# A planned two-layer transformer kernel: five groups of loads get other gates or places, and the order of work is planned anew with another price list

## The chip, the core and the metric

The kernel runs on one core of a Trainium2 chip. The core has a matrix engine (PE, with its weight loads shown apart as PEld), a vector engine (DVE), an activation engine (ACT), a general engine (POOL) and a queue engine (SP) that here issues every DMA. The metric is the device time of one execution in microseconds (us), the median of several.

## What is computed

Two sweeps of the same two layers over a sequence of 2048 tokens of width 576, all in bfloat16 at the edges:

```python
x = A_x                                              # 1 x 2048 x 576
for _ in range(2):
    y = layernorm(x)
    q, k, v = split(y @ wqkv)                        # 32 heads of 18
    p = softmax(where(0 <= i - j < 256, q k^T * 18**-0.5, -1e9))
    x = x + (p @ v) @ wo                             # sliding-block attention
    h = gelu_tanh(layernorm(x) @ w1 + b1)            # 576 -> 4608
    x = x + h @ w2 + b2                              # 4608 -> 576
```

## The kernel before

**Chunks and stages.** The 2048 tokens are cut in chunks of four tiles of 128 tokens; two sweeps give eight chunks, numbered k = 0 to 7. A chunk passes through: the first layernorm and a transpose of its tiles (`ln1_in`, `ln1`, written to `xnTa`), the q, k and v products (`qkv`), attention in eight groups of heads (`E0` for the first chunk, `E` for the others, cut in parts ea, eb and ec), the output product with the second layernorm and its transpose (`tail`, written to `xnTm`), and the MLP in three thirds of its 4608 hidden columns: `G_part` (first product and gelu: ga, gb, gc) and `mm2` (second product: ma, mb, mc). The MLP of chunk k-1 is woven with the attention of chunk k. A third of `w2` stays in `w2_sb` in two halves of 864 KB; `w1` goes through three slots, one slice of six column blocks each, of one load of 768 KB and two of 48 KB.

**The planner.** No order is written out by hand. Every instruction is added to a `Plan` as a task with its engine, the names it reads and writes, a cost, a latency (`lat`), for a DMA also a transfer time (`move`) and a number of descriptors (`desc`), and a priority. `Plan.schedule` then simulates the engines and at each step takes the task that can start first; among those of one starting time, the one of lowest priority number. A table `PL.nudge` adds a number to the priority of each stage by its name ("ga0" for the first third of chunk 0's MLP, "ga0+" for the weight loads that the stage issues, and so on). The order that comes out is the order of each engine's queue in the program; the engines then run it with semaphores, each strictly in its order. So the planned costs set the order, and never the time on the chip.

**DMAs and gates.** All DMAs are issued by SP, in the planned order. A load whose `reads` names something waits until that is written: this is a *gate*, though the load does not use the data. `dma_start_transpose` is a DMA that transposes a tile on its way: normalized tiles to `xnTa` and `xnTm`, and q and k tiles to `qT` and `kT`. Only chunk 0's normalized tiles and k tiles are transposed on PE (L738, L874). An SP instruction that waits holds all DMAs behind it.

**The start (the ramp).** SP loads token tiles 0 and 1, the q weights, tiles 2 and 3, the k weights, the v weights, then tiles 4 to 7. A DVE chain of fixed order (`PL.chain = "dv"`, L1149 to L1157) does the statistics of tile 0, half of tile 1's, the normalization of tile 0, the rest of tile 1's statistics, those of tile 2, then the normalization of tile 1, and so on. Then come `qkv` of chunk 0, its attention, and the first layernorm of chunk 1. PE fills planned gaps of over 0.4 us with products of zeros (`keep_warm`, L683).

**Names that the change touches.** The biases: `b1in` (a 36 x 128 view in `hT`) is loaded, transposed on PE (L1172) and copied to `b1col` (L1174); `b2bc` is loaded to all partitions. Both loads have the gate "k3", the fourth k tile of chunk 0. Gelu (L1086) reads `b1col`; POOL adds `b2bc` to `x_res` (L1092). Names used as gates: `k<i>` a transposed k tile, `v0h0` half of a v tile, `xa<i>` tile i of `xnTa`, `xm0_<i>` tile i of `xnTm` for an even chunk, `aq<g>` the attention output of head group g (L973), which is written once in each chunk. In the last chunk the third of `w2` that is used last goes to the place of `wqkv` (`w2x`).

Of the kernel before, what the change touches and what calls it, by code (L numbers as in the profile page):

```python
# [9 lines left out]
P = 128  # L10
# [176 lines left out]
class Plan:  # L187
# [75 lines left out]
    def schedule(self):  # L263
# [55 lines left out]
        served = {}  # L319
        n = len(self.tasks)  # L320
        while len(order) < n:
# [43 lines left out]
            if t.dma is not None:  # L365
# [15 lines left out]
                done = at + t.move  # L381
                for o in served:
                    if o != t.eng and served[o] > at:
                        both = min(t.move, served[o] - at)
                        served[o] += both
                        done += both
                served[t.eng] = done
                q.append((done - t.move, done, t.desc))
# [42 lines left out]
SWITCH = 0.095  # L431
TURN_FROM = 40.0
# [4 lines left out]
def build_kernel(nc, A_x, A_wqkv, A_wo, B_x, B_w1, B_b1, B_w2, B_b2, out):  # L437
# [42 lines left out]
    PL.nudge = {"": -230.72, "b": 275.87, "ea0.0": 68.12, "ea0.2": -36.73, "ea0.p0": 25.27, "ea0.p1": 8.39, "ea0.p2": 19.16,  # L480
# [168 lines left out]

    xin_load(0, 1)  # L650
    xin_load(1, 1)
    w_load(0)
    xin_load(2, 2)
    w_load(1)
    w_load(2)
# [660 lines left out]
```

## Time and profile before

| | |
|---|---|
| Median of 3 runs | 864.4 us (862.9 to 865.43) |
| The profiled execution's own time | 864.13 us |
| Its span, first to last instruction | 862.3 us |
| Granted PE clock, mean over the span | 0.998 |
| ACT busy | 593.2 us (69%) |
| DVE busy | 392.0 us (45%) |
| POOL busy | 377.9 us (44%) |
| DMA | 119.77 MB, 139 GB/s on average |

The profile is of one execution. Busy time is the time in which an engine has an instruction running; "PEclk" is the share of full clock that PE was granted. A timeline row gives the start, the duration, the engine, the line of the program, the operation with the tiles it writes and reads, and how many instructions were merged; in brackets stands the idle time before it and what ended it. Rows of stretches give the length, the busy time of each engine with its number of instructions, the granted clock, the share of the DMA engines and GB/s. In the chain of waits, each row says who waited, for whom, the total, the number of times and the longest.

### The profile page before, as it was taken

To read this page: it belongs to the slowest core of one execution; us is meant where nothing else is said; L and a number is where in the kernel's file an instruction comes from. 1 tells how busy PE (TensorE), PEld (TensorE's weight loads), DVE (VectorE), ACT (ScalarE), POOL (GpSimd) and SP (SyncE) were. 2 spreads that over 40 slices of the span, in tenths; PEclk is the share of its full clock that TensorE was granted. 3 is DMA by queue.
4 is the path that set the end of the run, shared out by engine and by line. 5 is a ranking of instruction groups with operands and counts; after the bars stand their busy time and mean duration, and the time that the engine had idled before them with its cause. 6 is when DMAs were issued, how large, how long until landed. Compare 5 with 4: busy or idle time off the path is not lost.

```text
span 862.3 us, 26990 instructions
## 1 busy us (share of the span) xinstructions
PE 848.7 (98%) x11578; PEld 520.5 (60%) x11578; DVE 392.0 (45%) x934; ACT 593.2 (69%) x741; POOL 377.9 (44%) x560
## 2 busy tenths in 40 slices
PE   8899999999999999999999999999999999999998
PEld 6556556656556565565655655656556656656656
DVE  7689424655228542384424832655224434243012
ACT  4796788768667588573875876737787589771730
POOL 4687544465135653264421863425454276222100
PEclk9999999999999999999999999999999999999999
DMA  7887435351583615957359443673536953355320
GB/s 192 197 193 142 124 125 148 109 163 44 166 181 107 163 43 166 204 93 169 90 151 218 92 139 125 116 177 98 173 112 119 289 155 105 126 166 146 120 83 28
DMA packets 181862, 119.77 MB, mean 139 GB/s; under 512 B 107440, under 2 KB 181744, under 8 KB 181744
## 3 DMA queue, kind: packets, MB, share of 16 engines
q1 hardware_dynamic: 181744, 118.05, 53.7%
q8 instruction: 91, 1.49, 0.7%
q14 instruction: 27, 0.22, 0.1%
HBM read 90.10 MB, written 2.36 MB: 107 GB/s over the span
## 4 chain that ended last, share of the span: by engine, by line
PE 87%; DMA 4%; DVE 4%; ACT 2%; issue 2%; SPq 1%; POOL 1%; POOLq 0%; DVEq 0%; ACTq 0%
PE ps L1076 31%; PE ps L781 27%; PE ps L784 9%; PE ps L840 8%; PE ps L909 6%; PE ps L956 4%; ACT pT L918 2%; DMA xnTm<-xn 2%; PE ps L800 1%; DMA xnTa<-xn 1%; DVE x_res L1019 1%; DVE xn L721 1%; DVE st_all L696 1%; SPq L633 1%; DMA wqkv<-in_A_wqkv_dram 1%
## 5 line engine op out<-in xcount | busy, mean ns | idle before, releaser
L939 POOL TENSOR_SCALAR_AFFINE_SELECT pT<-pT 128x512 bf16<-128x512 bf16 (+1 forms) x368 | 282.8, 789 | 250.1 <-ACT pT L918 244.9
L918 ACT ACTIVATE pT<-ps 128x1024 bf16<-128x1024 f32 (+1 forms) x384 | 345.1, 974 | 58.0 <-PE ps L909 57.6
L1076 PE MATMUL ps<-xnTm,w_sb 64*128 64x512 bf16 x2592 | 290.5, 376 | 0.9 <-DVE x_res L1019 0.3
L1086 ACT ACTIVATE hT<-ps,b1col 128x512 bf16<-128x512 f32 x276 | 167.4, 687 | 173.9 <-PE ps L1076 173.4
L1076 PEld LDWEIGHTS ps<-xnTm,w_sb 64*128 64x128 bf16 x2592 | 128.8, 94 | 142.5 <-issue 6.4
L781 PE MATMUL ps<-w_sb,hT 128*128 128x288 bf16 x1506 | 201.1, 287 | 0.0
L1019 DVE TENSOR_TENSOR x_res<-ps,x_res 128x288 f32<-128x288 f32 x224 | 100.0, 450 | 188.2 <-PE ps L781 162.1
L781 PEld LDWEIGHTS ps<-w_sb,hT 128*128 128x128 bf16 x1506 | 139.9, 98 | 51.5 <-issue 15.6
L840 PE MATMUL ps<-wqkv,xnTa 64*128 64x288 bf16 x1296 | 91.7, 283 | 1.6 <-DVE x_res L1019 1.1
L967 DVE STREAM_TRANSPOSE oq<-ps 128x512 f32<-128x512 f32 x64 | 45.8, 716 | 98.9 <-PE ps L956 98.0
L784 PE MATMUL ps<-w_sb,hT 128*32 128x288 bf16 x2424 | 83.7, 287 | 0.1
L861 DVE CAST qn<-ps 128x288 bf16<-128x288 f32 x120 | 49.0, 450 | 76.4 <-PE ps L840 68.8
L840 PEld LDWEIGHTS ps<-wqkv,xnTa 64*128 64x128 bf16 x1296 | 61.3, 94 | 31.4 <-issue 2.7
L784 PEld LDWEIGHTS ps<-w_sb,hT 128*32 128x32 bf16 x2424 | 62.2, 97 | 13.6 <-issue 4.2
L909 PE MATMUL ps<-qT,kT 32*128 32x384 bf16 (+2 forms) x1216 | 64.1, 276 | 2.8 <-ACT pT L918 2.3
L696 DVE BATCH_NORM_STATS2 st_all<-x_res 128x6 f32<-128x288 f32 (+1 forms) x128 | 53.4, 442 | 6.7 <-DMA x_res<-in_A_x_dram 5.8
L709 POOL TENSOR_SCALAR vtmp<-mv_all 128x1 f32<-128x1 f32 (+1 forms) x43 | 8.8, 204 | 107.7 <-DVE mv_all L700 105.3
L848 DVE CAST vA<-ps 128x288 bf16<-128x288 f32 x64 | 26.5, 450 | 63.2 <-PE ps L840 59.5
L1092 POOL TENSOR_TENSOR x_res<-x_res,b2bc 128x576 f32<-128x576 f32 x32 | 40.2, 1275 | 32.8 <-ACT hT L1086 32.8
L956 PE MATMUL ps<-pT,vA 128*20 128x384 bf16 (+2 forms) x1408 | 50.5, 276 | 0.2 <-DVE qn L861 0.2
L909 PEld LDWEIGHTS ps<-qT,kT 32*128 32x128 bf16 x1216 | 19.4, 92 | 42.8 <-issue 26.3
L781 PE MATMUL ps<-wo_sb,attT 128*128 128x288 bf16 x320 | 42.1, 287 | 0.3 <-DVE qn L861 0.3
(56 smaller groups left out, 465.1 us busy)
## 6 DMA issues: line engine op xcount, KB each, us to landing
w_sb<-in_B_w_dram SPq DMA_DIRECT2D x46, 864.0 KB, 6.0
w_sb<-in_B_w_dram SPq DMA_DIRECT2D x48, 768.0 KB, 4.7
w_sb<-in_B_w_dram SPq DMA_DIRECT2D x96, 48.0 KB, 4.4
wqkv<-in_A_wqkv_dram SPq DMA_DIRECT2D x3, 576.0 KB, 5.6
x_res<-in_A_x_dram SPq DMA_DIRECT2D x3, 576.0 KB, 5.7
wqkv<-in_B_w_dram SPq DMA_DIRECT2D x2, 864.0 KB, 6.3
out_dram<-x_res SPq DMA_DIRECT2D x12, 144.0 KB, 2.0
wo_sb<-in_A_wo_dram SPq DMA_DIRECT2D x4, 144.0 KB, 2.6
```

The source lines that it names most:

```text
L696: add("dve", lambda e, i=i, s=s: e.bn_stats(st_all[:, t, i, :], s[:, t, i * HB:(i + 1) * HB]), reads=res, writes=[f"st{t}_{i}"], cost=0.37 ...
L781: return e.matmul(bank(b)[:, 0:HB], lhs, rhs, start=start, stop=stop, skip_group_check=True)
L784: ins = e.matmul(bank(b)[32 * j:32 * j + 32, 0:HB], lhs[:, 32 * j:32 * j + 32], rhs, start=start, stop=stop, tile_position=(0, 32 * j), sk ...
L840: ins = e.matmul(bank(bs[o])[:, 0:HB], xnTa[r:r + 64, c, i * 128:(i + 1) * 128], wqkv[r:r + 64, c, col:col + HB], start=(c == 4), stop=(ph ...
L861: add("dve", lambda e, b=bs[o], dst=dst: e.tensor_copy(dst, heads_of(bank(b))), reads=[bs[o]], writes=[f"qn{sl}h{o}"], cost=0.375, lat=0.1 ...
L909: ins = e.matmul(two(bs[j // 2])[:, j % 2, col:col + nq * 128], k_of(T0 + so)[0][32 * j:32 * j + 32, g, :], qs[32 * j:32 * j + 32, g, qo * ...
L918: add("act", lambda e, h2=h2: e.activation(pT[:, sl, 2 * h2:2 * h2 + 2, lo:hi], two(bs[h2])[:, :, lo:hi], ACT.Exp, scale=SCALE), reads=[bs ...
L939: add("pool", lambda e, ap=ap, pat=pat, sgn=sgn, kind=kind: e.affine_select(ap, ap, pattern=pat, compare_op=(ALU.is_ge if kind == "d" else ...
L956: ins = e.matmul(bank(bo)[32 * j:32 * j + VW, qo * 128:(qo + nq) * 128], vA[:, (T0 + so) % VS, 8 * j + g, :], pT[:, sl, j, col:col + nq * ...
L1019: add("dve", lambda e: e.tensor_tensor(x_res[:, t, sl], bank(b)[:, 0:HB], x_old[:, t, sl], ALU.add), reads=[b] + ([f"xin{t}"] if first els ...
L1076: ins = e.matmul(bank(bks[i])[:, 0:n], w1_sb[r:r + 64, sls[i], col:col + 128], xnTm[r:r + 64, k % 2, c, 0:n], start=(c == 4), stop=(ph == ...
L1086: add("act", lambda e, ff=ff, hd=hd, bk=bk: e.activation(hd[:, 0:n], bank(bk)[:, 0:n], ACT.Gelu_apprx_tanh, bias=b1col[:, ff:ff + 1]), rea ...
```

## The change

It removes no arithmetic and adds none. It has six parts.

1. The three loads of the k weights go ahead of the load of token tiles 2 and 3.
2. The loads of both biases are moved from behind chunk 0's `qkv` (gate "k3") to a function `biases()` that is called after chunk 0's attention has been added (gate "aq1"); the PE transpose of b1 also waits for "aq7".
3. The second `w1` slice gets the gate of tiles 2 and 3 of `xnTa` in place of "v0h0", the third is moved to the MLP of chunk 0 with the gate of all four tiles of `xnTm` in place of "aq2".
4. The two halves of the first `w2` third get that same gate in place of "aq5" and "aq7".
5. The last `w2` third, in the place of `wqkv`, gets the gates "aq2" and "aq5" (of the last chunk).
6. The planner's price list: transposing DMAs get a longer latency and a shorter transfer, `w2` loads a shorter transfer, and a plain DMA of 500 descriptors or more that follows a transposing one while the queue is still busy is charged 0.8 more. With that the table of nudges is another; some of its entries (those of ea2, ea7, ga1 and ga6, for example) are those of before.

```diff
+                mv = t.move + (TURN_DMA if t.desc >= 500 and t.dma != "t" and turned.get(t.eng) and served.get(t.eng, 0.0) >= at else 0.0)
+                turned[t.eng] = t.dma == "t"
-                done = at + t.move
+                done = at + mv
...
+TURN_DMA = 0.8
...
-    PL.nudge = {"": -230.72, "b": 275.87, "ea0.0": 68.12, "ea0.2": -36.73, "ea0.p0": 25.27, "ea0.p1": 8.39, "ea0.p2": 19.16,
+    PL.nudge = {"": -92.05, "b": -19.76, "ea0.0": 28.56, "ea0.1": -4.45, "ea0.2": 114.56, "ea0.p0": -14.45, "ea0.p2": 33.51,
...
     w_load(0)
+    w_load(1)
     xin_load(2, 2)
-    w_load(1)
     w_load(2)
...
-            reads=rd, writes=[...], dma="t", ring=8, cost=1.3, lat=0.7, move=1.0, desc=640, prio=prio)
+            reads=rd, writes=[...], dma="t", ring=8, cost=1.3, lat=0.95, move=0.75, desc=640, prio=prio)
...
-                cls="w2", ring=NFH // WB, cost=0.55, lat=2.0, move=0.5 * WB,
+                cls="w2", ring=NFH // WB, cost=0.55, lat=2.0, move=0.4 * WB,
...
-                    reads=[f"qn{sl}h0", f"qn{sl}h1"], writes=[dn], dma="t", ring=8, cost=1.3, lat=1.1, move=1.3, desc=1024, prio=prio)
+                    reads=[f"qn{sl}h0", f"qn{sl}h1"], writes=[dn], dma="t", ring=8, cost=1.3, lat=1.4, move=1.0, desc=1024, prio=prio)
...
-    PL.stage = "b"
-    bb = Bank(FILL)
-    dma("sp", b1in, ..., reads=["k3"], writes=["b1i"], cls="b", ring=2, cost=0.5, prio=-1)
-    dma("sp", b2bc[:, :], ..., reads=["k3"], writes=["b2"], cls="b", ring=2, cost=0.5, prio=-1)
-    add("pe", lambda e: e.transpose(...), reads=["b1i", "ident"], writes=[bb], cost=0.1, lat=0.22, prio=5, alloc=[bb])
-    add("dve", lambda e: e.tensor_copy(b1col[:, :], ...), reads=[bb], writes=["b1"], cost=0.1, lat=0.14, prio=5)
...
+    def biases():
+        PL.stage = "b"
+        bb = Bank(FILL)
+        dma("sp", b1in, ..., reads=["aq1"], writes=["b1i"], cls="b", ring=2, cost=0.5, prio=-1)
+        dma("sp", b2bc[:, :], ..., reads=["aq1"], writes=["b2"], cls="b", ring=2, cost=0.5, prio=-1)
+        add("pe", lambda e: e.transpose(...), reads=["b1i", "ident", "aq7"], writes=[bb], cost=0.1, lat=0.22, prio=5, alloc=[bb])
+        add("dve", lambda e: e.tensor_copy(b1col[:, :], ...), reads=[bb], writes=["b1"], cost=0.1, lat=0.14, prio=5)
...
             PL.stage = f"ga{k - 1}"
+            if k == 1:
+                w1_load(-1, [f"xm0_{i}" for i in range(4)])
             G_part(k - 1, 0, b + 0.6)
         if k == 1:
-            w2_load(0, 1, ("aq5", "aq7"))
+            w2_load(0, 1, [[f"xm0_{i}" for i in range(4)]] * 2)
...
             if k == 0:
-                w1_load(-1, ["v0h0"])
-                w1_load(-1, ["aq2"])
+                w1_load(-1, ["xa2", "xa3"])
+                biases()
...
-            w2_load(2, b + 3, k=k - 1)
+            w2_load(2, b + 3, ("aq2", "aq5") if k == NK else None, k=k - 1)
```

More of the change, by code (lines that the diff above doesn't have):

```diff
@@ L319, in schedule @@
         served = {}
+        turned = {}
         n = len(self.tasks)
@@ L380, in schedule @@
                 at = max(served.get(t.eng, 0.0), st + t.cost + min(t.lat, 2.0))
-                done = at + t.move
+                mv = t.move + (TURN_DMA if t.desc >= 500 and t.dma != "t" and turned.get(t.eng) and served.get(t.eng, 0.0) >= at else 0.0)
+                turned[t.eng] = t.dma == "t"
+                done = at + mv
                 for o in served:
                     if o != t.eng and served[o] > at:
-                        both = min(t.move, served[o] - at)
+                        both = min(mv, served[o] - at)
                         served[o] += both
@@ L387, in schedule @@
                 served[t.eng] = done
-                q.append((done - t.move, done, t.desc))
+                q.append((done - mv, done, t.desc))
                 done += max(0.0, t.lat - 2.0)
@@ L744, in ln_norm_T @@
         add("sp", lambda e: e.dma_start_transpose(dst[:, :, i * 128:(i + 1) * 128], xn[:, sl, :]),
-            reads=rd, writes=[f"{dname}{i}"] + (["kx0", "kx1"] if dname == "xm1_" else []), dma="t", ring=8, cost=1.3, lat=0.7, move=1.0, desc=640, prio=prio)
+            reads=rd, writes=[f"{dname}{i}"] + (["kx0", "kx1"] if dname == "xm1_" else []), dma="t", ring=8, cost=1.3, lat=0.95, move=0.75, desc=640, prio=prio)
     w1n = [0]
@@ L774, in w2_load @@
             dma("sp", wt[:, WB * b:WB * b + WB, :], B_w2[f0 * P:(f0 + WB) * P, :].rearrange("(w p) d -> p w d", p=P),
-                reads=[gate[b]] if gate else [], writes=[f"{wn}{b}"] + ([f"w{w}{x}{h}" for w in "qkv" for x in "BC" for h in range(2)] + [f"w{w}A" for w in "qkv"] if wn == "w2x" else []), cls="w2", ring=NFH // WB, cost=0.55, lat=2.0, move=0.5 * WB,
+                reads=([gate[b]] if isinstance(gate[b], str) else gate[b]) if gate else [], writes=[f"{wn}{b}"] + ([f"w{w}{x}{h}" for w in "qkv" for x in "BC" for h in range(2)] + [f"w{w}A" for w in "qkv"] if wn == "w2x" else []), cls="w2", ring=NFH // WB, cost=0.55, lat=2.0, move=0.4 * WB,
                 desc=128 * WB, prio=prio)
@@ L1165, in build_kernel @@
     PL.part = ""
-    PL.stage = "b"
-    bb = Bank(FILL)
-    dma("sp", b1in, bass.AP(tensor=B_b1.tensor, offset=B_b1.offset, ap=[[P, NF], [1, P]]), reads=["k3"], writes=["b1i"], cls="b", ring=2,
-        cost=0.5, prio=-1)
-    dma("sp", b2bc[:, :], bass.AP(tensor=B_b2.tensor, offset=B_b2.offset, ap=[[0, P], [1, D]]), reads=["k3"], writes=["b2"], cls="b", ring=2,
-        cost=0.5, prio=-1)
-    add("pe", lambda e: e.transpose(bank(bb).bitcast(BF16)[:, 0:NF], b1in, ident[0:NF, 0:NF]), reads=["b1i", "ident"], writes=[bb],
-        cost=0.1, lat=0.22, prio=5, alloc=[bb])
-    add("dve", lambda e: e.tensor_copy(b1col[:, :], bank(bb).bitcast(BF16)[:, 0:NF]), reads=[bb], writes=["b1"], cost=0.1, lat=0.14, prio=5)
     PL.stage = ""
@@ L1197, in wo_load @@
             dma("sp", wo_sb[32 * j:32 * j + 16, 4, :], A_wo[r + 128:r + 144, :], reads=["aq0"], writes=[f"woB{j}"], cls="wo", cost=0.6)
+    def biases():
+        PL.stage = "b"
+        bb = Bank(FILL)
+        dma("sp", b1in, bass.AP(tensor=B_b1.tensor, offset=B_b1.offset, ap=[[P, NF], [1, P]]), reads=["aq1"], writes=["b1i"], cls="b", ring=2,
+            cost=0.5, prio=-1)
+        dma("sp", b2bc[:, :], bass.AP(tensor=B_b2.tensor, offset=B_b2.offset, ap=[[0, P], [1, D]]), reads=["aq1"], writes=["b2"], cls="b", ring=2,
+            cost=0.5, prio=-1)
+        add("pe", lambda e: e.transpose(bank(bb).bitcast(BF16)[:, 0:NF], b1in, ident[0:NF, 0:NF]), reads=["b1i", "ident", "aq7"], writes=[bb],
+            cost=0.1, lat=0.22, prio=5, alloc=[bb])
+        add("dve", lambda e: e.tensor_copy(b1col[:, :], bank(bb).bitcast(BF16)[:, 0:NF]), reads=[bb], writes=["b1"], cost=0.1, lat=0.14, prio=5)
     later = [k for k in range(2, NK) if CH[k][0] == 0]
```

140 rows, old and new, of the table add are left out of this document.

## Prediction

> **What bounds the kernel now.** I read the page's busy times first, then the busy time by stretches, the waits, and the timelines of PE, SP and ACT where PE idles.
>
> ```profile
> span 862.3 us, 26990 instructions
> ...
> PE 848.7 (98%) x11578; PEld 520.5 (60%) x11578; DVE 392.0 (45%) x934; ACT 593.2 (69%) x741; POOL 377.9 (44%) x560
> ```
>
> PE is the bound: 862.3 - 848.7 = 13.6 us without a matmul. By the stretches PE lacks 3.1 us in 0 to 20, 3.0 in 20 to 40, 1.2 in 40 to 60, 1.3 in 60 to 120 and, added up from the 20 us rows, 2.0 in all of 140 to 800. The last product ends at 859.4, so 2.9 us are the output's way out. A change of order can win little after 140 us; the ramp is where it is.
>
> ```profile
> 29.46 0.35 PE L909 MATMUL ps<-qT,kT 32*128 32x256 bf16 x8 [0.38 <-DVE mv_all L700]
> 30.72 0.34 PE L909 MATMUL ps<-qT,kT 32*128 32x384 bf16 x4 [0.91 <-ACT pT L918]
> 32.48 2.59 PE L784 MATMUL ps<-wqkv,xnTa 128*32 128x288 bf16 x40 [1.42 <-DMA xnTa<-xn]
> 34.86 0.77 PE L956 MATMUL ps<-pT,vA 128*20 128x384 bf16 x16
> 35.55 0.34 PE L909 MATMUL ps<-qT,kT 32*128 32x256 bf16 x8
> ```
>
> PE stands 1.42 us for a tile of chunk 1 that a transposing DMA brings; the scores of chunk 0 (35.55) stand in its queue behind that product. The clock falls meanwhile:
>
> ```profile
> 31.00:31.50 0.50, 0.06 (x4) 0.00 (x0) 0.48 (x2) 0.50 (x2) 0.07 (x1) 1.00 0.08 9
> 31.50:32.00 0.50, 0.00 (x0) 0.00 (x0) 0.00 (x0) 0.50 (x2) 0.50 (x1) 0.65 1.03 326
> 32.00:32.50 0.50, 0.02 (x4) 0.02 (x6) 0.00 (x0) 0.50 (x2) 0.50 (x1) 0.50 1.05 292
> ...
> 34.50:35.00 0.50, 0.50 (x16) 0.34 (x12) 0.00 (x0) 0.00 (x0) 0.50 (x2) 0.50 0.52 165
> 35.00:35.50 0.50, 0.50 (x20) 0.21 (x11) 0.37 (x1) 0.00 (x0) 0.10 (x1) 0.94 0.00 0
> ```
>
> The column before the last two is the granted clock: 0.50 from about 31.65 to 35.05. ACT pays:
>
> ```profile
> 29.85 2.92 ACT L918 ACTIVATE pT<-ps 128x768 bf16<-128x768 f32 x4 [0.56 <-PE ps L909]
> 35.95 23.16 ACT L918 ACTIVATE pT<-ps 128x768 bf16<-128x768 f32 x32 [3.18 <-PE ps L909]
> ```
>
> From 35.95 to 64.05 ACT idles 0.18 us: chunk 0's attention is bound by its exponentials. So the 3.18 us of ACT idle are on the path, not only PE's 1.42. SP shows why the tile was late:
>
> ```profile
> 21.66 0.60 SPq L633 DMA_DIRECT2D hT<-in_B_b_dram  x1
> 22.36 1.24 SPq L880 DMA_TRANSPOSE qT<-qn  x1
> 23.70 2.02 SPq L744 DMA_TRANSPOSE xnTa<-xn  x1
> 25.77 0.58 SPq L633 DMA_DIRECT2D b2bc<-in_B_b_dram  x1
> 26.45 2.52 SPq L744 DMA_TRANSPOSE xnTa<-xn  x2
> 29.02 0.57 SPq L633 DMA_DIRECT2D w_sb<-in_B_w_dram  x1
> 29.64 2.29 SPq L744 DMA_TRANSPOSE xnTa<-xn  x1
> ```
>
> The four tiles were normalized by 20.5 (DVE's and POOL's timelines), but stand behind w1's first slice, tiles 8 to 11, both biases and, the last one, w1's second slice. The chain of work that ended last takes the one issued at 27.70, which landed 4.74 us later.
>
> **The sum, part by part.**
>
> *Biases (part 2) and w1's second slice (part 3): -2.5.* The bias issues ahead of that tile cost 0.60 and 0.58 with gaps of 0.10 each: 1.38 us that SP gives back, and 153 KB less ahead of it. The 1.42 us wait all but goes. With it goes the slow clock: 40 products in 2.59 against 2 x 0.80 for 20 of the same kind at 38.69 and 41.44, so 0.99, and 0.11 on the P.V product (0.77 against 0.66). 1.4 + 1.1 = 2.5, of ACT's 3.18. Bounds: 0 if another DMA comes late in its place; -4.0 if the 0.38 + 0.91 + 0.20 us beside it go too (2.91 + 1.10). I take 2.5, since those are waits for ACT, which is busy then. What the biases now cost: two issues of 1.2 us after 41.8 (group 1's output), one PE transpose of 0.19 and a copy of 0.18 after 66.3; gelu first reads b1 at 90.31, POOL b2 at 91.14. Over 20 us of cover; without it, 0.2 plus the wait. w1's second slice, behind the tiles, is first used some 4 us into the MLP at 87: covered. SP is also rid of 1.77 us (w1's third slice, 49.13) and 0.97 (w2, 57.79 and 66.69) there.
>
> *k weights ahead of tiles 2 and 3 (part 1): +0.3.* 648 KB (0.66 MB) at the 329 to 334 GB/s of 4 to 8 us make 2.0: the tiles land near 10.0 where DVE now has them at 7.96; the k weights land 288 KB, 0.9 us, before 10.16. DVE's fixed chain puts tile 1's normalization (8.93) behind tile 2's statistics, so it slips 2 us, and q of tile 1 with it. Tile 2, which the first scores need, is normalized at 10.43 but transposed on PE only at 12.74, behind a product that waited for the k weights: 1.5 us of slack. q of tile 2 is copied out at 16.39, behind statistics of tiles 4 to 7 whose landing (13.28) doesn't move. Bounds: -0.9 (k weights earlier, all of it on the path) to +2.0; most of the slip is absorbed, so +0.3.
>
> *w1's third slice and w2's first third behind xnTm (parts 3, 4): 0.* At 86.7 SP now issues tiles 12 to 15 (576 KB, landed after 4.3 us, at 91.0). Behind them now come 864 + 1728 = 2592 KB, 2.65 MB. At 366 GB/s (row 96 to 98) they land at 98.3, at 272 (100 to 102) at 100.8. w2's first half is needed at 99.82, after 11.83 us of first products that start from the same tiles, the second some 0.8 later. It just fits, and both ends move with the tiles. Bounds 0 and +7.5, the first rival.
>
> *The last w2 third (part 5): 0.* Its loads go out at 671.94 and 679.25 and are used after 835; PE has no idle time in 660 to 700, so nothing is won.
>
> *The order found anew (part 6): -1.1.* In the ramp ACT also waits 0.67 and 0.56 for scores (27.79, 29.85); longer transposes in the plan make it put such products later: half of 1.23, -0.6. After 140 a quarter of the 2.0 idle, -0.5 (the largest is 1.07 before 389.47, for a tile of xnTm). What a new order does to PE's turns between kinds of product is not to be read; one turn costs 0.1: 20 products take 2.56 and 192 take 23.64 in the chain, so 2.56 - 20 x 0.123. Twenty turns more or fewer, of the chain's 756 pieces, bound it at +2.0 and -2.0; I take none.
>
> Sum: 864.13 - 2.5 + 0.3 - 1.1 = 860.8, against its own span 859.0 and 1.8 around it; the median of the runs lies 0.27 above the profiled one, which I leave. About 0.3% (2.6 us: 861.8 to 867.0) is what a measurement here tells from no change.
>
> **The rivals.**
>
> *Late MLP weights (slower).* Everything gathered behind xnTm meets the transposes of chunk 1's q and k. Such stretches ran at 147 (84 to 88) and 196 GB/s (96 to 100). At their mean, 172, the 2.65 MB take 15.4 us and land at 106.4: 5.8 us behind the need, and the clock's fall costs half of 3.4: 860.8 + 7.5 = 868.3. It decides below 2.65 MB / (100.6 - 91.0) = 276 GB/s. For it: no spare landing place; against: 366 and 358 GB/s (116 to 120) in weight loads alone, and 92 to 96 nearly free of DMA.
>
> *The gain is lost at the start.* Tiles 2 and 3 come 2.0 later and the first scores with them: 860.8 + 1.7 = 862.5, no change by the bound. For it DVE's fixed chain; against it the 1.5 us of slack.
>
> *The clock falls all the same.* PE is thinly used from 29.0 on, before the wait: 1.5 of the 3.4 us up to 31.65. If the wait goes and the fall stays, 1.1 is not won: 861.9. [...]
>
> *All small waits go too.* -4.0, +0.3, all of 1.23 and 0.8 of 2.0 idle: 858.4.
>
> *The new order turns more often.* 40 turns: 864.8. Nothing speaks for or against it.
>
> **How the numbers follow.** The forecast 0.46, its own range 859.3 to 862.3 (0.42 of it faster, 0.04 within); late weights 0.23, slower; the start 0.09, within; the clock 0.06, half faster; all waits 0.11, faster; turns 0.05, 0.03 within, 0.02 slower. Faster 0.56, within 0.3% 0.19, slower 0.25. The range 857.5 to 867.5 leaves out the worse half of the late weights and the best of the order.
>
> **What would show it.** Right: no DMA wait of PE near 30, clock 1.00 from 28 to 36, no ACT gap above 1 us from 22 to 60, chunk 0's MLP starting 2 to 3 us before 87.07, no wait of PE on w_sb near 97, busy PE in 140 to 800 as before. Wrong: first scores past 22 us; a wait on w_sb between ga0 and the first mm2; PE busy grown by over 1 us.

## The result and the profile after

| | before | changed |
|---|---|---|
| Median of 15 runs | 864.29 us (861.87 to 865.76) | 862.04 us (861.8 to 862.79) |
| The profiled execution's own time | 864.13 us | 861.97 us |
| Granted PE clock, mean over the span | 0.998 | 1.000 |

The ratio of changed to before is 0.9981, 95% interval 0.9973 to 0.9989. By the medians that is 2.25 us less, by the ratio 1.6 us (1.0 to 2.3); 3.3 were forecast. The changed kernel is faster, by less than the 0.3% that the prediction called no change. Before's times fall in two groups, as the experiments show, and its median lies in the slower one, so the difference of the medians is the less firm. The changed kernel's line numbers stand four higher here than before's (L784 is now L788).

The page's span and busy times, after:

```profile
span 860.3 us, 27204 instructions
...
PE 849.0 (99%) x11684; PEld 521.0 (61%) x11684; DVE 393.9 (46%) x934; ACT 594.1 (69%) x741; POOL 377.9 (44%) x560
```

PE still bounds the kernel; its 11.3 us without a matmul are 2.3 fewer than before. PE's timeline where it had stood 1.42 us, and ACT's beside it:

```profile
30.18 1.40 PE L804 MATMUL ps<-wqkv,xnTa 128*128 128x288 bf16 x10
31.51 0.34 PE L913 MATMUL ps<-qT,kT 32*128 32x384 bf16 x4
31.78 1.41 PE L788 MATMUL ps<-wqkv,xnTa 128*32 128x288 bf16 x40
33.24 0.67 PE L960 MATMUL ps<-pT,vA 128*20 128x384 bf16 x16
33.84 0.34 PE L913 MATMUL ps<-qT,kT 32*128 32x256 bf16 x8
```

```profile
28.22 5.20 ACT L922 ACTIVATE pT<-ps 128x768 bf16<-128x768 f32 x7
34.23 23.50 ACT L922 ACTIVATE pT<-ps 128x768 bf16<-128x768 f32 x32 [0.82 <-PE ps L913]
```

The 40 products follow without a wait and take 1.41 us in place of 2.59; ACT's gap is 0.82 in place of 3.18. SP's queue shows why:

```profile
20.67 3.04 SPq L748 DMA_TRANSPOSE xnTa<-xn  x2
...
28.46 2.56 SPq L637 DMA_DIRECT2D w_sb<-in_B_w_dram  x3
31.11 2.55 SPq L748 DMA_TRANSPOSE xnTa<-xn  x2
...
40.15 0.36 SPq L637 DMA_DIRECT2D hT<-in_B_b_dram  x1
40.55 0.37 SPq L637 DMA_DIRECT2D b2bc<-in_B_b_dram  x1
```

The biases go out at 40; no bias load stands among the transposes any more. But the start is slower. PE and DVE, after, in the first 12 us, and PE where chunk 0's MLP begins; then three rows of before:

```profile
10.74 0.60 PE L687 MATMUL ps<-warm 128*128 128x256 bf16 x4
...
11.93 0.44 PE L742 MATMUL ps<-ident,xn 128*128 128x128 bf16 x5
...
86.33 11.83 PE L1080 MATMUL ps<-xnTm,w_sb 64*128 64x512 bf16 x108
98.08 0.92 PE L788 MATMUL ps<-w_sb,hT 128*32 128x288 bf16 x24
```

```profile
10.01 0.82 DVE L700 BATCH_NORM_STATS2 st_all<-x_res 128x6 f32<-128x288 bf16 x2 [0.75 <-DMA x_res<-in_A_x_dram]
...
11.22 0.38 DVE L725 TENSOR_SCALAR xn<-x_res,mv_all,rstd 128x576 bf16<-128x576 bf16 x1
```

```profile
8.93 0.38 DVE L721 TENSOR_SCALAR xn<-x_res,mv_all,rstd 128x576 bf16<-128x576 bf16 x1
...
21.16 0.34 PE L909 MATMUL ps<-qT,kT 32*128 32x384 bf16 x4
...
87.07 11.83 PE L1076 MATMUL ps<-xnTm,w_sb 64*128 64x512 bf16 x108 [0.29 <-DVE attq L973]
```

Tile 1 is normalized at 11.22 (8.93 before), PE multiplies zeros meanwhile, and the MLP begins at 86.33, only 0.75 before the old 87.07, though 2.6 us of stall and slow clock are gone. By then PE has done the same work in both kernels. Adding its rows up from start to start (worked out from the trace): its idle time fell from 7.4 to 5.6, its zeros grew from 5.4 to 7.4, and its products went from 73.2 to 72.4. From the first MLP product to the last PE instruction, 772.3 us became 770.9.

Stretches of 20 us (length; busy time and instructions of PE, PEld, DVE, ACT, POOL; granted clock, DMA share, GB/s), after and then before:

```profile
20.00:40.00 20.00, 18.25 (x260) 11.07 (x262) 14.49 (x39) 18.62 (x28) 13.38 (x23) 1.00 0.87 193
...
380.00:400.00 20.00, 20.00 (x300) 11.13 (x300) 8.77 (x20) 14.42 (x21) 13.43 (x19) 1.00 0.67 178
```

```profile
20.00:40.00 20.00, 16.99 (x224) 10.59 (x221) 11.66 (x33) 14.77 (x22) 11.06 (x18) 0.91 0.92 200
...
380.00:400.00 20.00, 18.83 (x256) 11.38 (x256) 12.53 (x29) 10.29 (x15) 11.50 (x17) 1.00 0.74 152
```

The rows of 380 to 400 hold the longest wait behind the ramp in before, which is gone:

```profile
389.47 1.28 PE L840 MATMUL ps<-wqkv,xnTa 64*128 64x288 bf16 x18 [1.07 <-DVE x_res L1019]
```

PE stood there for a residual addition of DVE (L1019), not for a tile of xnTm, as the prediction read it.

### The profile page after: what moved, and what is told of

It is laid out like the page before. It is cut to its first block, busy times and chain, and to the rows that moved or that the text cites. A ratio compares the mean times of both kernels' runs of the same rounds, so it can differ in the third digit from the quotient of the medians.

```text
span 860.3 us, 27204 instructions
## 1 busy us (share of the span) xinstructions
PE 849.0 (99%) x11684; PEld 521.0 (61%) x11684; DVE 393.9 (46%) x934; ACT 594.1 (69%) x741; POOL 377.9 (44%) x560
## 4 chain that ended last, share of the span: by engine, by line
PE 93%; ACT 3%; issue 1%; DVE 1%; SPq 1%; DMA 1%; POOL 0%; POOLq 0%
PE ps L1080 33%; PE ps L785 30%; PE ps L788 9%; PE ps L844 9%; PE ps L913 6%; PE ps L960 5%; ACT pT L922 2%; SPq L637 1%; DMA x_res<-in_A_x_dram 1%; PE ps L804 1%; ACT kT L882 0%; POOL pT L943 0%; DVE oq L971 0%; DVE x_res L1023 0%; ACT hT L1090 0%
## 5 line engine op out<-in xcount | busy, mean ns | idle before, releaser
L785 PE MATMUL ps<-w_sb,hT 128*128 128x288 bf16 x1482 | 198.4, 287 | 0.0
L785 PEld LDWEIGHTS ps<-w_sb,hT 128*128 128x128 bf16 x1482 | 137.4, 98 | 51.2 <-issue 15.8
L788 PE MATMUL ps<-w_sb,hT 128*32 128x288 bf16 x2520 | 87.9, 287 | 0.5 <-ACT hT L1090 0.5
L788 PEld LDWEIGHTS ps<-w_sb,hT 128*32 128x32 bf16 x2520 | 64.8, 97 | 14.0 <-issue 3.9
```

The source lines that it names most:

```text
L785: return e.matmul(bank(b)[:, 0:HB], lhs, rhs, start=start, stop=stop, skip_group_check=True)
L788: ins = e.matmul(bank(b)[32 * j:32 * j + 32, 0:HB], lhs[:, 32 * j:32 * j + 32], rhs, start=start, stop=stop, tile_position=(0, 32 * j), sk ...
```

## The experiments

The question was which part gains and which gives back. The main theory: the late biases gain, the early k weights give back, and a fall of the clock sits in before's time. The rival: the new order makes the gain, or all parts do little.

**The kernel before, unchanged.** No edit.

> The kernel before, unchanged, to see each execution's clock beside its time. Theory F (the clock falls only in some executions): the executions fall in two groups, mean granted clock 1.000 with 862 to 863 us and 0.998 with 864 to 866 us. Rival (the clock falls near 31.65 in every execution, the spread is of something else): 0.998 in all of them, at any time.

864.07 us, ratio 1.0008 (0.9997 to 1.002). What matters is inside it: seven of its twelve executions had a mean clock of 0.998 or less and a median of 865.06, five had full clock and 863.29. All 123 executions of the unchanged kernel beside the experiments split so: 55 at full clock, median 862.87; 60 at 0.998, median 864.93; 8 at 0.996, median 866.84. So about half of the executions have a fall of the clock, and with one they take 2.1 us longer in the median. A clock of 0.50 over 3.41 us can account for at most 1.7 of that; what makes the rest is not shown. Before's median, by its time, is that of an execution with a fall, as was the profiled one.

The control's profiled execution had a fall too, from 32.31 to 35.72, but behind a shorter wait:

```profile
31.91 2.25 PE L784 MATMUL ps<-wqkv,xnTa 128*32 128x288 bf16 x40 [0.64 <-DMA xnTa<-xn]
```

PE waited 0.64 us here and 1.42 in the first profile, yet the MLP began at 87.33, later than 87.07. In the first profile 0.83 us of the slow stretch passed while PE stood still, in this one none. So the wait and the fall, which overlap, did not simply add up here.

**Only the biases late** (before's order otherwise):

```diff
-order: ... qkv of chunk 0, b1 load, b2 load, ... PE transpose of b1, its copy ...
+order: ... last load of wo, b1 load, b2 load, ... PE transpose of b1, its copy, first MLP product
```

> The planned order of before on every engine, with the two bias loads alone moved in SP's queue, behind the loads of wo (and b1's transpose and copy just ahead of chunk 0's MLP). Theory M (the prediction's first term): no wait of PE near 32, clock 1.000, 1.5 to 2.5 us faster than before, 862 to 862.8. Theory E (the ramp ends by something else, as the 0.75 us by which the changed kernel's MLP starts earlier suggests): the wait goes but at most 0.7 us are won, 863.6 or more.

862.49 us, ratio 0.9989 (0.998 to 0.9999). PE's timeline:

```profile
30.94 0.34 PE L909 MATMUL ps<-qT,kT 32*128 32x384 bf16 x4 [0.91 <-ACT pT L918]
31.21 1.41 PE L784 MATMUL ps<-wqkv,xnTa 128*32 128x288 bf16 x40
...
84.86 11.83 PE L1076 MATMUL ps<-xnTm,w_sb 64*128 64x512 bf16 x108
```

The wait and the fall are gone; the MLP begins at 84.86, 2.2 before 87.07. Ten of eleven executions had full clock; their median, 862.47, is only 0.4 below that of before's undisturbed executions in the same session (862.84).

**Only the k weights first** (before's order otherwise):

```diff
-load q weights, load tiles 2 and 3, load k weights
+load q weights, load k weights, load tiles 2 and 3
```

> The planned order of before on every engine, with the load of token tiles 2 and 3 alone moved behind the k weights in SP's queue. Theory M (+0.3, absorbed): 0 to 0.5 us slower than before. Theory Z (the later tiles hold back the first scores, and PE fills up with zeros or idles): 0.8 to 2 us slower. Rival (earlier k weights help): up to 0.9 faster.

866.79 us, ratio 1.0035 (1.0023 to 1.0048): 3.0 us slower by the ratio, more than any of the three expected. PE's timeline:

```profile
10.77 0.50 PE L738 MATMUL ps<-ident,xn 128*128 128x128 bf16 x5 [1.71 <-DVE xn L721]
...
22.18 0.34 PE L909 MATMUL ps<-qT,kT 32*128 32x384 bf16 x4
```

PE waits 1.71 us for tile 1's normalization, the first scores slip from 21.16 to 22.18 and the MLP from 87.07 to 88.58. All five executions had a fall and three of them, by a mean clock of 0.996, two: 1.6 on average against before's 0.6 (76 falls in 123).

**The changed kernel with tiles 2 and 3 first again**, all else, its order too, kept.

> The changed kernel with its planned order on every engine, with the load of token tiles 2 and 3 alone put back ahead of the k weights in SP's queue. Theory M: 0 to 0.5 us faster than the changed kernel, 861.5 to 862.0. Theory Z: 0.8 us or more faster, 861.2 or less, first scores below 21. Rival (the order on PE is now made for early k weights, whose product comes first): slower, 862.5 or more, with a wait of PE on the k weights near 10.

862.79 us, ratio 0.9989 (0.9979 to 1.0): nothing won back. PE's timeline:

```profile
10.20 1.39 PE L804 MATMUL ps<-wqkv,xnTa 128*128 128x288 bf16 x10 [0.93 <-DMA wqkv<-in_A_wqkv_dram]
```

PE's new order has a k product here and now waits for its weights. The changed order is made for early k weights; undoing that part alone only moves the wait, and the MLP begins at 86.71, not earlier than 86.33.

**Start of one kernel, rest of the other.** The order of every engine was written out: up to the first MLP product from one kernel, behind it from the other. In three such kernels a gate came from the other kernel:

> Everything up to the first product of chunk 0's MLP in the order of before, everything behind it in the order of the changed kernel; both have done the same products on PE by then. Theory S (the two parts add up; the profiles give -0.75 us to that point and -1.5 behind it): 1.3 to 1.5 us faster than before, 0.9983 to 0.9985, and the clock still falls in about half of the executions. Rival (the new rest is only good behind its own ramp): no faster than before.

> The other half: up to chunk 0's MLP the order of the changed kernel, behind it that of before. Theory S: 0.7 us faster than the executions of before without a fall, clock 1.000 in nearly all, 862.2 to 863.0. Theory F (the ramp's gain is the clock's fall alone): no faster than the executions of before at clock 1.000 (862.8 in the median of the first four experiments' runs of before), but rarely slower than 863.5.

> Up to chunk 0's MLP the order of before with the two bias loads moved behind the loads of wo, behind it the order of the changed kernel. Theory S: the 1.06 us of the late biases and the 1.3 to 1.5 of the rest add up, 2.4 us faster than before (0.9972), and faster than the changed kernel by 0.3 to 1 us, since its ramp gives up what the early k weights cost. Rival (only one of them counts, both end in the same wait): no faster than the changed kernel.

868.82 us (1.0054, 1.0034 to 1.0075), 865.0 (1.0009, 0.9997 to 1.0022) and 867.27 (1.0032, 1.0018 to 1.0047). They say nothing of the question: in this program a gate is a read, so whoever next writes the named tile must wait for the gated load. With the late biases SP stood 4.0 us for a `w_sb` load before it could issue a transpose at 33.49, and all DMAs behind with it. With before's start the MLP began at 92.2, with the late biases at 89.3. They were done anew, each load with the gate of the kernel that its place came from:

```diff
-    S.add(t.eng, t.fn, names(t.reads), names(t.writes), ...)
+    S.add(t.eng, t.fn, names(GATES.get(n, t.reads)), names(t.writes), ...)
...
+GATES = {323: ('k3',), 324: ('k3',), 325: ('b1i', 'ident'), 320: ('v0h0',), 321: ('v0h0',), 322: ('v0h0',), 515: ('aq2',), ...
```

**The changed kernel again**, in the same session:

> The changed kernel unchanged, on the same chip as the three others: 0.9981 of before, clock 1.000 in nearly all executions.

862.22 us, ratio 0.9982 (0.997 to 0.9993). Eleven of twelve executions had full clock (median 862.14); the profiled one had a fall and took 864.59.

**Before's start, the changed rest:**

> As h_before_after (order of before up to chunk 0's MLP, that of the changed kernel behind it), but each load has the gate of the kernel that its place comes from. Theory W (in the h kernels a gate named a tile that in the other order is written only later, so that the writer waited for the load to land, 5 us in the ramp): ramp as before, 87.1 to 87.4 with the clock's fall, rest 771, in all 1.3 us faster than before, 0.9985, with two groups by the clock. Rival (the rest needs its own ramp): as h_before_after, slower than before.

863.4 us, ratio 0.9986 (0.9973 to 0.9998). Its profiled execution has before's wait without before's fall:

```profile
32.22 1.41 PE L788 MATMUL ps<-wqkv,xnTa 128*32 128x288 bf16 x40 [1.44 <-DMA xnTa<-xn]
...
85.93 11.83 PE L1080 MATMUL ps<-xnTm,w_sb 64*128 64x512 bf16 x108 [0.65 <-DVE vA L852]
```

The same wait, the products at full speed, the MLP at 85.93. By these profiles, of the 2.2 us in the ramp 1.1 (87.07 - 85.93) are the fall and 0.9 to 1.1 the wait (85.93 against 85.06, below, and 84.86). The split is rough: the two executions are not typical, since this one took 863.68 where those at full clock have a median of 862.73, and before's took 864.13 where those with one fall have 864.93.

**The changed start, before's rest:**

> As h_after_before (the changed ramp, the order of before behind it), with the gates of the kernel that each place comes from. Theory S: 0.7 us faster than the executions of before at clock 1.000 (862.9 in all so far), so 862.2, and clock 1.000 in nearly all. Theory F: as the executions of before at clock 1.000, 862.9.

864.28 us, ratio 1.0 (0.9989 to 1.0011). All twelve at full clock, yet slower than both theories had it. The seam between the two parts adds waits of its own (1.9 us of issue and 0.9 for DVE, in a profiled execution of 866.46), and the MLP begins at 87.60, where the changed kernel has 86.33, so this run does not price the start. The changed kernel's own 86.33 against the 85.93 above does: its start is no faster than before's without a fall.

**Before's start with late biases, the changed rest:**

> As h_late_after (order of before with late biases up to chunk 0's MLP, order of the changed kernel behind it), with the gates of the kernel that each place comes from. Theory S: 2.4 us faster than before (0.9972) and 0.3 to 1 us faster than the changed kernel. Rival (late biases help only against the clock's fall, and the changed ramp does that as well): as the changed kernel, 0.9981.

861.87 us, ratio 0.9973 (0.9962 to 0.9984), all eleven at full clock. PE's timeline at the start and at the MLP:

```profile
9.05 0.51 PE L742 MATMUL ps<-ident,xn 128*128 128x128 bf16 x5 [0.36 <-DVE xn L725]
...
85.06 11.83 PE L1080 MATMUL ps<-xnTm,w_sb 64*128 64x512 bf16 x108 [0.72 <-DVE vA L852]
```

The MLP begins 1.3 us before that of the changed kernel without the early k weights. Behind it 1.1 us are lost again (771.9 against 770.9), presumably since the rest was planned for another start; that was not tested.

**The same with the k weights first**, one DMA moved (8 is the load of tiles 2 and 3):

```diff
-ORDER = (..., 4, 19, 31, 20, 8, 32, 21, 33, 5, 36, 34, 35, 6, 7, 37, ...)
+ORDER = (..., 4, 19, 31, 20, 32, 21, 33, 5, 36, 34, 35, 6, 7, 8, 37, ...)
```

> g_late_after (late biases up to chunk 0's MLP, the changed kernel's order behind it) with the load of token tiles 2 and 3 behind the k weights. Theory P (part 1 is what the changed ramp gives back): the MLP of chunk 0 starts at 86.0 to 86.5 instead of 85.07, first scores 1 us later, 1 to 1.5 us slower than g_late_after, 0.9985 to 0.999 of before. Theory M (the prediction: +0.3, absorbed): 0.9973 to 0.9977. If it is no slower, the changed ramp's 1.3 us are the new order's and not the tiles'.

864.97 us, ratio 1.0012 (0.9998 to 1.0026), against 0.9973 without the move. PE's timeline and its stretches:

```profile
11.49 0.56 PE L742 MATMUL ps<-ident,xn 128*128 128x128 bf16 x5 [2.83 <-DVE xn L725]
...
24.34 0.34 PE L913 MATMUL ps<-qT,kT 32*128 32x384 bf16 x4
```

```profile
9.00:11.50 2.50, 0.01 (x1) 0.01 (x1) 1.39 (x5) 0.03 (x1) 0.25 (x1) 1.00 1.08 362
11.50:12.00 0.50, 0.50 (x6) 0.45 (x7) 0.50 (x2) 0.50 (x2) 0.43 (x1) 0.71 0.74 260
12.00:13.00 1.00, 1.00 (x6) 0.61 (x5) 0.93 (x4) 0.74 (x3) 0.37 (x2) 0.50 0.20 71
13.00:15.00 2.00, 2.00 (x11) 1.23 (x9) 1.21 (x2) 0.71 (x3) 1.22 (x2) 0.50 0.62 119
```

PE stands 2.83 us for tile 1 and the clock then falls, from 11.70 to 15.12: there is no fall near 31 any more, but one near 11. Nine of twelve executions had a fall somewhere. The three at full clock took 863.0 to 863.8, so the slip alone costs some 1.2 us over 861.87 (of another session) and the falls the rest.

**w1's second slice late, beside the biases** (on before, and on the late biases with the changed rest, the best start):

> b_biases_late with the three loads of w1's second slice moved behind chunk 1's four transposed tiles too, all else in the order of before. Theory M (prediction: that slice stood in the same way): the last tile comes some 0.6 us earlier, 0 to 0.6 us faster than b_biases_late, 0.9982 to 0.9989, clock 1.000 in all. Rival (after the biases nothing waits for those tiles any more): as b_biases_late, 0.9989.

> g_late_after with w1's second slice behind chunk 1's four transposed tiles too. Theory M (it stood in the way of the last tile): 0.2 to 0.6 us faster than g_late_after, 0.9966 to 0.9971. Rival (b_bias_w1_late gave 862.39 at full clock against 862.47 of b_biases_late: nothing): 0.9973.

862.52 us (0.998, 0.9968 to 0.9993); full-clock executions 862.39, with the biases alone 862.47. On the best start 862.27 (0.9987, 0.9974 to 0.9999), the MLP at 85.22 against 85.06. The slice adds nothing that can be told.

**The first scores earlier**, by a q copy of DVE moved ahead:

> g_late2_after with q of tile 2 copied out on DVE ahead of the statistics of tiles 6 and 7, and the first scores one product earlier on PE. Theory A (chunk 0's attention is bound by its exponentials, so the path begins at the first scores): first scores near 20.4 instead of 21.2, 0.5 to 0.8 us faster than g_late2_after. Rival (PE has the same products to do before chunk 0's MLP and no gap to close by that): no faster, within 0.2 us.

861.89 us (0.9981, 0.9966 to 0.9995). The first scores come at 20.43 in place of 21.37, the MLP at 85.12 in place of 85.22: 0.9 us there is worth 0.1 later. The medians differ by 0.4, with intervals that overlap. When the first scores start does not by itself set the ramp.

## Why the prediction was off

The direction was right, the size was not: 3.3 us were forecast, and 2.25 by the medians or 1.6 by the ratio measured. Of the prediction's own signs of being right one failed, the MLP that starts 2 to 3 us before 87.07: it starts 0.75 before. In the profile no sign of being wrong came; the first scores, at 21.35, stayed below 22.

**Biases and w1's second slice, -2.5: right for an execution with a fall, too much over all of them.** The wait and the fall went together and the MLP came 2.2 us earlier with the biases alone. The slice's share is nothing that shows. "1.4 + 1.1" was measured between single profiles as about 1.0 for the wait and 1.1 for the fall, between the groups of whole times as 0.4 and 2.1. And the fall comes in 68 of 123 executions of the unchanged kernel only; the term counted it in full. So the late biases alone have a ratio of 0.9989, 1.0 us, and with the slice, in another session, 0.998, 1.7 us. One profile could not tell that.

In these traces the low stretch lasted 3.4 us (31.65 to 35.06 before, 32.31 to 35.72 in the control, 11.70 to 15.12 with the k weights moved, 11.38 to 14.80 in the changed kernel again), and the same program has a fall in some executions and none in others (68 and 55 of before's 123). The length of the wait alone does not decide it: PE waited 1.42 us in before and 0.64 in the control, with a fall each time, and 1.44 in before's start with the changed rest, where the clock held. What makes the clock fall in one execution and not in another is not shown.

**The k weights ahead of tiles 2 and 3, +0.3: the step that failed most.** "Most of the slip is absorbed" was wrong. The landing near 10.0 and the 2 us slip of tile 1 came as forecast, but tile 1's slip was given no price, and the 1.5 us of slack counted for tile 2 did not cover it: in before's order PE's queue has tile 1's transposes ahead of the products that follow (1.71 and 2.83 us of wait). Moved alone, the part costs 3.0 us on the kernel before and 0.0039 of the ratio (3.4 us, between two sessions) on the best start, 1.0 to 1.5 by the slip and the rest by more falls. The rival "the gain is lost at the start" (+1.7) had the right place, but it let the first scores come 2.0 later; alone they came 1.0 later and in the changed kernel 0.2 (21.35). It too priced no fall.

**In the changed kernel 1.3 to 1.5 us are lost at the start.** Its newly planned PE order puts k products and zeros where tile 1 is awaited, and only one of its 27 listed executions has a fall (a mean clock of 0.998): there PE stood 2.09 us for the k weights at 10.44, and the clock fell at 11.38. But its MLP begins at 86.33, where the late biases alone reach 84.86 and 85.06. Nearly all of that is lost before the first scores: until then PE spends 8.4 us on zeros and idle time in the changed kernel, against 7.2 with the late biases alone, 7.1 in before and 8.3 with the k weights first (worked out from the traces). That the loss is of the size that the early k weights make by themselves speaks for the slip. How much of it is the slip and how much the new order itself was still not taken apart: with tiles 2 and 3 first again the same order spends 8.7.

**The order, -1.1: the sum near by luck, both halves misplaced.** The -0.6 in the ramp is not there (PE's waits for ACT before scores went from 2.3 us, in the kernel with late biases alone, to 1.9; the zeros grew by 1.9). Behind the ramp -0.5 was forecast and the profiles show -1.5: 0.6 less idle, the wait before 389.47 above all, 0.4 of zeros gone, and 0.4 less in products. There are 495 changes between kinds of products in place of 510 (counted by the line and tiles of successive products); at the 0.1 a turn that the prediction worked out they would make 1.5, and products became only 0.4 shorter. By whole times it is less sure: before's start with the changed rest has 0.9986, but its full-clock executions (862.73) are only 0.2 below before's (862.92), with a seam wait of 1.8 us for a tile of xnTm in its profile.

**MLP weights behind xnTm, 0: right.** The first product with w2 starts at 98.08 without a wait, and PE's list of waits names no `w_sb`. The rival with most weight (868.3) did not happen. The last w2 third: nothing shows.

In the profiled executions, then: -2.2 for the biases, +1.5 for k weights and order in the ramp (86.33 - 84.86) where -0.3 was forecast, -1.5 behind it where -0.5 was; together -2.2, and the spans differ by 2.0. The median of 862.04 lies within the forecast's own range of 859.3 to 862.3 only because the gain behind the ramp was three times its term. The kernel with late biases and the changed rest stands at 0.9973, the changed kernel at 0.9981 and 0.9982. It beats the kernel before; that it beats the changed kernel is not shown, since the intervals overlap.

## What to carry to other kernels

Before a stall is priced from one profile, look at the clock of many executions of the same program: here the stall was 1.42 us, the clock fell in 68 of 123 executions, and those with one fall took 2.1 us longer in the median. One stall removed while another is opened can bring a fall back elsewhere: with the k weights moved PE stood 2.83 us, and the clock fell at 11.70 in place of 31.65. Price a load that is moved back on the first instruction of each strictly ordered engine that stands behind it, not on the slack of the latest user: here PE stood 1.71 us for tile 1 while tile 2's 1.5 us of slack had been counted. In a program like this one, a gate on a load is also a hold on the next writer of what it names (SP stood 4.0 us behind one here).

## What the runs showed that was not expected

The clock's fall comes in 55% of the executions of one unchanged program. Executions with one take 2.1 us longer in the median, more than the 1.7 that half speed over 3.41 us can make and than the 1.1 between two single profiles; the difference stays open. PE did not always stand still when the clock fell. In the control its products had begun again at 31.91 and the clock fell at 32.31; in the kernel with late biases and the k weights moved PE had stood 2.83 us, was at work again at 11.49, and the clock fell at 11.70. In the kernel before the clock fell while PE stood, at 31.65. The first products of zeros were also slow for a varying time: one took 417 ns up to a start at 4.0 us in before's trace and at 6.3 in the changed kernel's, and 273 ns soon after.
